# Strassen's scheme for the last 2048 tokens in two blocks, rows of x by head pairs through DRAM, and a third T tile

## The chip, the cores and the metric

The kernel runs on one core of a Trainium2 chip. The metric is the device time of one execution in microseconds (us), and the time of a kernel is the median of its runs. Engines are named as in the profile: PE (matmul), PEld (its weight loads), DVE (vector), ACT (scalar), POOL (GpSimd) and SP, which only issues DMAs here.

## The reference

Eight batches of eight heads, 576 positions, head size 64. Causal attention with a decay, then a feed-forward layer with a softplus over all 4608 tokens. Everything is float32.

```
scores = scale * np.matmul(q, k.transpose(0, 1, 3, 2))
cum = np.cumsum(np.log(np.clip(f, 0.0001, 1.0)), axis=-1)
scores = np.where(causal, -1000000000.0, scores + cum[:, :, :, None] - cum[:, :, None, :])
attn = softmax(scores)                       # exp(scores - max) / (sum + 1e-09)
x = matmul(attn, v) as [4608, 512]           # token by (head, head size)
h = x @ w_in                                 # 512 -> 2048
g = np.maximum(h, 0.0) + np.log1p(np.exp(-np.abs(h)))
out = g @ w_out                              # 2048 -> 512
```

## The kernel before

**Precision.** A product of two float32 matrices is made of three matmuls on rounded halves: high by high, high by low, low by high. So nearly every operand is first split: a copy gives the high part (`h`, ACT or DVE), and a subtraction gives the low part (`l`, DVE). Where a name ends in `h` or `l`, this is meant.

**Attention.** One job is one head of one batch. The first 14 jobs (batch 0, `plain`) are built otherwise; the other 56 (`whole`, batches 1 to 7, eight jobs each) are alike. A job loads q and k (`raw`) and v (`vr`), splits v into `vhl` (L785 is its low part), and builds a T tile [128, 4, 576]: the high part of q and k, the low part (L811), four moves of 144 KB inside SBUF (L814) and rows of the decay (L802, L805). It then makes scores in six pieces: two matmuls each (L859, L860) into a PSUM bank of the tag `att`, of which there are four, the row minimum with mask on DVE (L864) and the exponential on ACT (L903). The weights are scaled (L931, L933), turned by PE (L996), split into `ph` and `pl` (L1015, L1018), and multiplied with v (L1143). The result is added into x on ACT and DVE (L1193). Two T tiles take turns, by the job's number.

**x.** One batch of x is a tile [128, 4, 576]: plane g holds the heads 2g and 2g + 1, and 576 tokens. There are two such buffers (`x32`); they also hold the running sums of the decay at the start and the gated values of the last block at the end.

**Feed-forward.** The first 3584 tokens go in blocks: two of 128, one of 256 and six of 512 tokens (`WIDE`). A wide block splits x (L1285), makes 16 up products of 12 matmuls with 512 columns each (L1336, weights `wih` in SBUF and `wl` loaded per pair from DRAM), a gate of three ACT passes (L1369, L1372, L1375), a sum on DVE (L1383) and a split (L227, L1391), and 16 down products (L1423), of which half the tokens' values wait in DRAM (`g_d`, L1395 out, L1478 back) for a second pass. So a wide block is 192 up and 192 down matmuls.

**The last 1024 tokens** (`SUPER, NSUPER = 1024, 1`) are one block by Strassen's scheme in Winograd's form. Even and odd tokens are two halves of 512. Per pair of 128 hidden columns (`fp`, eight pairs) seven products of six matmuls stand where eight stood (L1856, banks A, B, C, D), with sums of weight quarters on POOL (L1738), sums of products on DVE (L1885) and four gates. The down products of the even tokens (L1978, banks E0 to E3) follow at once; the gated values of the odd tokens go to DRAM (`odd_d`, L1929) and come back in a tail (L2012) after the last product. `lay_x` makes the seven operands B11, T2, T1, T3, B21, B22, T4 from x in SBUF. They lie in tiles that attention has left (`late_raw`, `late_T`, `late_vhl`, `late_ph`, `late_pl`, `late_p`, `late_xl`).

**The order.** All engines' instructions are put in an order by a planner (`Plan.run`) with a cost for each operation; the engines then run their queues in that order and wait by semaphores. Operations wait in it for buffers by tag (`takes`, `give`), mostly first come first served. Feed-forward units are dealt out between the parts of the attention jobs by `share`. The last pass of the last wide block (`left`) stands between attention and the Strassen block.

## Time and profile before

| what | us |
|---|---|
| median of 3 runs (1135.66 to 1136.82) | 1136.08 |
| the profiled execution | 1137.25 |
| its span | 1135.4 |
| PE busy in the span | 1123.0 |
| DVE busy | 850.8 |
| ACT busy | 838.8 |
| POOL busy | 185.6 |

A row of a group reads: line, engine, operation, out<-in, partitions by elements, count, busy us, mean ns of one. The chain of waits names what the end of the program was waiting for at each moment. In a table by stretch, each engine has its busy us and, in brackets, its number of instructions. A matmul's record lasts longer than its share of PE, since the next begins before it ends; the distance of starts is the share.

### The profile page before, as it was taken

What the parts mean: (1) busy time and instruction counts of PE and PEld (TensorE: products, weight loads), DVE (VectorE), ACT (ScalarE), POOL (GpSimd) and SP (SyncE); (2) the same over time, 40 slices, a digit from 0 to 9 for tenths busy, and PEclk for the clock granted to TensorE, in tenths of its full rate; (3) what the DMA queues carried; (4) which work ended last, traced back from release to release, by engine and by line L of the source; (5) the groups of instructions that cost most, each with busy time, mean ns of one, the idle gap of its engine ahead of it and who ended that gap; (6) DMA issues with size and microseconds to landing.
All of it is one profiled execution on the core that took longest, in us unless ns stands there. A gap on an engine that the chain in (4) does not pass through costs nothing.

```text
span 1135.4 us, 19910 instructions
## 1 busy us (share of the span) xinstructions
PE 1123.0 (99%) x6230; PEld 939.8 (83%) x6230; DVE 850.8 (75%) x2131; ACT 838.8 (74%) x2033; POOL 185.6 (16%) x225
## 2 busy tenths in 40 slices
PE   9999999999999999999999999999999999999998
PEld 7766789888888888888888888888888888888887
DVE  7888999987787777777777778677867778867610
ACT  6888798889877777678767787677867875766610
POOL 3323221111111001000010000000000013555200
PEclk9999999999999999999999999999999999999999
DMA  8868676566575656666576466665657535322481
GB/s 244 252 183 229 179 215 163 148 174 175 158 208 159 174 164 175 161 186 170 151 203 189 137 179 182 165 179 158 174 153 208 142 99 162 130 93 98 162 278 38
DMA packets 160489, 192.97 MB, mean 170 GB/s; under 512 B 54944, under 2 KB 120768, under 8 KB 160384
## 3 DMA queue, kind: packets, MB, share of 16 engines
q1 hardware_dynamic: 160216, 191.55, 59.1%
q8 instruction: 50, 0.82, 0.3%
q14 instruction: 55, 0.45, 0.1%
q10 hardware_dynamic: 168, 0.15, 0.0%
HBM read 114.17 MB, written 44.34 MB: 140 GB/s over the span
## 4 chain that ended last, share of the span: by engine, by line
PE 86%; DVE 8%; ACT 3%; DMA 2%; issue 1%; SPq 0%; DVEq 0%
PE acc L1423 24%; PE h L1336 24%; PE b L996 7%; PE o L1143 7%; PE late_E L1978 4%; PE s L860 4%; PE s L859 4%; PE late_A L1856 2%; PE late_D L1856 2%; PE late_C L1856 2%; DVE s L864 1%; PE late_B L1856 1%; PE late_D L1978 1%; PE late_C L1978 1%; PE late_A L1978 1%
## 5 line engine op out<-in xcount | busy, mean ns | idle before, releaser
L864 DVE CUSTOM_DVE_ANT_0 s<-s,cmask 128x288 f32<-128x288 f32 (+6 forms) x320 | 137.1, 440 | 60.6 <-PE s L860 54.2
L903 ACT ACTIVATE pb<-s,negm 128x288 f32<-128x288 f32 (+5 forms) x272 | 143.3, 531 | 45.8 <-DVE negm L864 43.9
L933 POOL TENSOR_SCALAR pb<-pb,rsum 128x448 f32<-128x448 f32 (+2 forms) x44 | 59.5, 1353 | 415.8 <-ACT e L1375 192.9
L1336 PE MATMUL h<-xh,wl 128*128 128x512 f32 (+1 forms) x448 | 126.0, 380 | 0.0
L1336 PE MATMUL h<-xh,wih 128*128 128x512 f32 (+1 forms) x448 | 117.0, 383 | 0.5 <-DVE gl L1391 0.5
L1018 DVE TENSOR_TENSOR pl<-b,ph 128x512 fp32r<-128x512 f32 x168 | 107.1, 662 | 9.5 <-ACT ph L227 8.7
L1336 PE MATMUL h<-xl,wih 128*128 128x512 f32 (+1 forms) x448 | 113.9, 376 | 0.0
L227 ACT CAST ph<-b 128x512 fp32r<-128x512 f32 (+2 forms) x169 | 80.1, 492 | 34.8 <-PE b L996 33.1
L859 PE MATMUL s<-T 128*128 128x192 f32 (+1 forms) x336 | 99.3, 304 | 3.0 <-ACT pb L903 1.3
L1423 PE MATMUL acc<-woh_dt_float32r,gh 128*128 128x512 f32 x248 | 99.2, 400 | 0.0
L1369 ACT ACTIVATE e<-h 128x512 f32<-128x512 f32 x112 | 66.8, 596 | 43.3 <-PE h L1336 42.2
L860 PE MATMUL s<-T 68*128 68x192 f32 (+1 forms) x336 | 98.2, 296 | 0.0
L1423 PE MATMUL acc<-woh_dt_float32r,gl 128*128 128x512 f32 x248 | 97.4, 393 | 0.0
L1423 PE MATMUL acc<-wol_dt_float32r,gh 128*128 128x512 f32 x248 | 97.1, 392 | 0.0
L1336 PEld LDWEIGHTS h<-xl,wih 128*128 128x128 f32 x448 | 80.8, 188 | 16.6
L1336 PEld LDWEIGHTS h<-xh,wl 128*128 128x128 f32 x448 | 80.1, 189 | 13.0 <-issue 0.5
L1383 DVE SCALAR_TENSOR_TENSOR h<-h,e 128x512 f32<-128x512 f32 x104 | 73.3, 705 | 20.4 <-ACT e L1375 19.4
L1336 PEld LDWEIGHTS h<-xh,wih 128*128 128x128 f32 x448 | 77.8, 189 | 11.8 <-DVE gl L1391 0.7
L1143 PE MATMUL o<-ph,vhl 128*128 128x512 f32 x336 | 84.8, 290 | 0.0
L1391 DVE TENSOR_TENSOR gl<-h,gh 128x512 fp32r<-128x512 f32 x104 | 71.5, 687 | 16.0 <-ACT gh L227 14.6
L996 PE MATMUL b<-halves,pb 128*128 128x128 f32 x512 | 82.2, 272 | 0.0
L1372 ACT ACTIVATE e<-e 128x512 f32<-128x512 f32 x112 | 70.8, 632 | 1.9
(368 smaller groups left out, 2812.9 us busy)
## 6 DMA issues: line engine op xcount, KB each, us to landing
T<-T SPq DMA_DIRECT2D x224, 144.0 KB
wl<-wil_d SPq DMA_DIRECT2D x56, 512.0 KB
raw<-in_qkT SPq DMA_DIRECT2D x112, 144.0 KB
g_d<-gh SPq DMA_DIRECT2D x84, 128.0 KB
g_d<-gl SPq DMA_DIRECT2D x84, 128.0 KB
vr<-in_vR SPq DMA_DIRECT2D x64, 160.0 KB
out<-ob SPq DMA_DIRECT2D x28, 256.0 KB
sto<-in_w_out SPq DMA_DIRECT2D x11, 512.0 KB
```

Source lines behind the costliest of these rows:

```text
L227: (e.tensor_copy if hasattr(e, "tensor_copy") else e.copy)(out, in_)
L859: e.matmul(o, qA[:, S - end : S - q0], kA[:, a:z], start=True, stop=False)
L860: e.matmul(o, qB[0:ST, S - end : S - q0], kB[0:ST, a:z], start=False, stop=True)
L864: e.tensor_tensor_reduce(out=box["o"], in0=box["o"], in1=cmask[0:n_q, right - w : right], scale=-0.125, scalar=m0 if i else 3.0e38, op0=AL ...
L903: e.activation(o, box["o"], AF.Exp, bias=m1, scale=-1.0, accum_out=acc)
L996: e.transpose(box["ps"][0 : x.shape[1], at : at + one.shape[1]], x, one)
L1018: e.tensor_sub(box["l"], box["ps"][:, 0:w], box["h"].bitcast(F32))
L1143: e.matmul(boxes[gi]["ps"][0:m, a:z], st["vhl"][:, c, 0:m], pbox[which][:, o : o + z - a], start=gi in fresh and which == "h", stop=gi == ...
L1336: e.matmul(o, l, r, start=m == 0, stop=m == 11)
L1423: e.matmul(st["acc", tt], l, r[fc], start=first and m == 0, stop=last and m == 2,)
L1856: e.matmul(banks[to], stationary(x, j), at(b, y, j), start=start and m == 0, stop=m == 5, skip_group_check=not start,)
L1978: e.matmul(banks[x], l, r[fc], start=first and m == 0, stop=final and m == 2)
```

## The change

Strassen's scheme takes the last 2048 tokens, in two blocks of 1024, and the wide blocks are four and no longer six. The x of batches 2 to 7 is no longer kept by batches in SBUF: a buffer `xc` holds four planes (`xp`), an attention job writes into the plane of its head pair, and after every second job `store_x` sends that plane to DRAM (`x_d`, 288 KB). The wide blocks from token 1024 on load their x back by planes (256 KB, `split_stored`), and each Strassen block loads its x in two loads of 1 MB (`lay_x`). The other x buffer (`x0`) becomes a third T tile once batch 0 has been used. After attention both buffers (`big`) are used by turns for the loaded x of a Strassen block and for its gated even values. T tiles are taken as they come free. The low parts of T and `vhl` may now be made on POOL too. The tail of the first block takes the banks E0 and E1 for its second half, and its last eight units come after the second block's preparation, the last five of them ranked behind (`FILL`, `BEHIND`). The planner's costs for a DMA, and the shares by which feed-forward units are dealt out, are others.

```diff
-SUPER, NSUPER = 1024, 1
-BEHIND = 190
+SUPER, NSUPER = 1024, 2
+POOLB = 0.0
+BEHIND, FILL, REST, START = 190, 5, 4, 3
...
-                x32=2, ps=2, wl=2, vhl=3, vraw=1, raw=2, one=2)
-    plan = Plan(BUFS | dict(T0=4, stat=4, p=2, xh0=1, xh1=1, xl0=1))
+                xc=1, x0=1, ps=2, wl=2, vhl=3, vraw=1, raw=2, one=2)
+    plan = Plan(BUFS | dict(T0=4, xp=0, big=0, stat=4, p=2, xh0=1, xh1=1, xl0=1))
...
-            vl = add(subs(nv * D), v_lo, after=[vh])
+            vl = add([subs(nv * D), On("POOL", 0.2 + nv * D * 0.0022, POOLB, True)], v_lo, after=[vh])
...
-                t = T[number % 2]
+                st["at"] = T_free.pop(0)
+                t = T[st["at"]]
...
-            l_ = add(On("DVE", 0.75, 0.0, True), lo, after=[h_])
+            l_ = add([On("DVE", 0.75, 0.0, True), On("POOL", 0.2 + S * 0.0022, POOLB, True)], lo, after=[h_])
...
-            give("T", st["scores"])
+            give("T", st["scores"], lambda: T_free.append(st["at"]))
...
+    def store_x(b, g):
+
+        def store(e):
+            e.dma_start(out=x_d[g, :, b * S : (b + 1) * S], in_=plane(b, g))
+
+        need = [d for _, _, d, g_ in wrote[b] if g_ == g]
+        stores[b, g] = add_dma(store, 288, after=need)
+        if b > 1:
+            done = add(NO_ENGINE, mark, after=[stores[b, g]])
+            give("xp", [done], lambda: xp_free.append(x_of[b, g]))
...
+        def split_stored():
+            ready, low = [], []
+            for cc in range(NCC):
...
+                    e.dma_start(out=box["x"], in_=x_d[cc, :, t0 : t0 + nt])
...
+                if b == 0 and lo + w == S:
+                    give("x0", splits[0])
+                    third = add(NO_ENGINE, mark, takes=("x0",), lag=0.0)
+                    set_rows(2, [third])
+                    give("T", T_set[2], lambda: T_free.append(2))
...
+            give("big", [add(NO_ENGINE, mark, takes=("xp",) * NCC, lag=0.0)], lambda: big_free.append("xc"))
+            give("big", [add(NO_ENGINE, mark, takes=("T",), lag=0.0)], lambda: big_free.append("x0"))
...
+                def load(e, j=j, xbox=xbox):
+                    xbox["at"] = big_free.pop(0)
...
+                    e.dma_start(
+                        out=xbox["x"],
+                        in_=x_d[j : NCC : 2, :, t0 : t0 + SUPER].rearrange("c p t -> p c t"),
+                    )
+
+                ld = add_dma(load, 1024, after=stored(t0, SUPER, (j, j + 2)), takes=("big",))
...
+                if fc in (NFC - 3, NFC - 1):
+                    k = fc // 2 % 2
+                    give("big", [o], lambda: big_free.append(g_room["at", k]))
...
-            one = tail(["B", "A"], 0, False)
-            two = tail(["C", "D"], 2 * P, s == NSUPER - 1)
+            end = s == NSUPER - 1
+            spots = [(x, j) for x in OPERANDS[: 7 if end else 2] for j in range(2)]
+            one = tail(["B", "A"], 0, spots, False)
+            two = tail(["E0", "E1"], 2 * P, spots, end)
...
-        share = sum(c for c, _ in ffn) / (until - n + 1 + DELAY) / max(1, len(units))
+        here = sum(c for c, _ in ffn)
+        share = here / (until - n + 1 + (START if n <= nstart + H else DELAY))
...
+        whole_ = n - 1 - nstart
+        if n > nstart and whole_ % 2 == 1:
+            store_x(1 + whole_ // H, whole_ % H // 2)
...
-        for i, (_, unit) in enumerate(left):
-            plan.late = BEHIND * (i >= len(left) - 5)
+        for i, unit in enumerate(left):
+            plan.late = BEHIND * (i >= len(left) - FILL)
             unit()
-        plan.late, left = 0, []
-        for unit in units:
+        plan.late, left = 0, units[len(units) - 8 :]
+        for unit in units[: len(units) - 8]:
             unit()
+    for unit in left:
+        unit()
```

Two places show the order of the queues. The first is SP's queue where attention ends and the first Strassen block begins: `gh`/`gl` are the loads of the last wide block's second pass, `x_d` is x in DRAM, `late_x` the loaded x of a Strassen block, `late_wl` its weights. Before, the block's x is in SBUF and nothing is loaded for it:

```order
L1722 DMA late_wl0_1_11361<-wil_d_96 128x1024
L1478 DMA gh8_0b_11416<-g_d_97 128x2x256
L1478 DMA gl8_0b_11418<-g_d_97 128x2x256
L1235 DMA out_0<-ob8_0_11432 128x512
L1235 DMA out_0<-ob8_1_11443 128x512
L1478 DMA gh8_1b_11511<-g_d_97 128x2x256
L1478 DMA gl8_1b_11513<-g_d_97 128x2x256
```

Now, in SP's queue at the same place, the last plane of batch 7 is stored and the second load of x comes behind two more loads of the second pass:

```order
L1563 DMA gh6_3b_10279<-g_d_97 128x2x256
L1563 DMA gl6_3b_10281<-g_d_97 128x2x256
L1248 DMA x_d_98<-xp_2909 128x576
L1563 DMA gh6_4b_10335<-g_d_97 128x2x256
L1563 DMA gl6_4b_10337<-g_d_97 128x2x256
L1563 DMA gh6_5b_10360<-g_d_97 128x2x256
L1563 DMA gl6_5b_10362<-g_d_97 128x2x256
L1720 DMA late_x2560_1_10365<-x_d_98 128x2x1024
L1563 DMA gh6_6b_10383<-g_d_97 128x2x256
```

What moved: the store of x and the two loads of x are new in this queue, and the second load stands between the loads that PE's cover needs.

The second place is PE's queue where a Strassen block's first product stands (`late_A` to `late_D` are its banks, `acc` and `late_E` those of down products). Before, there is one such place, behind the second pass of the last wide block:

```order
L1423 MATMUL acc8_3_11494<-woh9_dt_float32r_1523,gh8_4b_11610 128x512
L1423 MATMUL acc8_3_11494<-wol9_dt_float32r_1555,gh8_4b_11610 128x512
L1423 MATMUL acc8_3_11494<-woh9_dt_float32r_1523,gl8_4b_11612 128x512
L1856 MATMUL late_A_11380<-late_raw1_10993,wih_95 128x512
L1856 MATMUL late_A_11380<-late_T0_11158,wih_95 128x512
```

Now PE's queue has a second such place: the second block's first product (bank C) stands in the first block's tail, whose values `gho` have come back from DRAM:

```order
L2058 MATMUL late_A_10028<-woh13_dt_float32r_1577,gho0_0_6_11570 128x512
L2058 MATMUL late_A_10028<-wol13_dt_float32r_1909,gho0_0_6_11570 128x512
L2058 MATMUL late_A_10028<-woh13_dt_float32r_1577,glo0_0_6_11572 128x512
L1937 MATMUL late_C_10288<-late_T1_10018,late_xh0_10005 128x512
L1937 MATMUL late_C_10288<-late_vhl0_10088,late_xh0_10005 128x512
```

What moved: this product was nowhere before, and 36 matmuls of the first block's tail stand between it and the first block's last down product.

More of the change, by code (lines that the diff above doesn't have):

```diff
@@ L95, in start_of @@
             n, free = op.takes.count(tag), self.free[tag]
-            early = self.queue[tag][0] is not op
+            head = self.queue[tag][0]
+            early = 0 if head is op else head.takes.count(tag) if EARLY else 1
             if len(free) < n + early or (early and not op.loose):
+                return None
+            if early and op.guard and op.guard.end is None:
                 return None
@@ L126, in run @@
                 op.lag = SEEN[eng]
+            if op.kb:
+                self.moved = max(self.moved, op.start + ISSUE) + op.kb / RATE
+                op.lag = max(0.0, self.moved - op.end) + LAND
             if on.port:
@@ L1218, in attention, with plane, stored @@
         )
-    splits = {}
+    splits, stores = {}, {}
+    def plane(b, g):
+        return x_of[b][:, g, :] if b < 2 else xp["x"][:, x_of[b, g], :]
+    def store_x(b, g):
[6 more added lines that the diff above has]
+            give("xp", [done], lambda: xp_free.append(x_of[b, g]))
+    def stored(t0, n, planes=range(NCC)):
+        return [stores[b, g] for b in range(t0 // S, (t0 + n - 1) // S + 1) for g in planes]
     kept_read = {}
@@ L2036, in step @@
                     loads["used", fp].append(o)
+                    if not spots_of[fp] and tiles[-1] == k == 1:
+                        give("gh", [o])
+                        give("gl", [o])
                     return o
@@ L2242, in tile_decay_attention_softplus_ffn @@
         until = min((at for at in ready_at if at >= n), default=n)
-        share = sum(c for c, _ in ffn) / (until - n + 1 + DELAY) / max(1, len(units))
+        here = sum(c for c, _ in ffn)
+        share = here / (until - n + 1 + (START if n <= nstart + H else DELAY))
+        if n > nstart + H:
+            later = sum(NFC * on_pe(WIDE, 24).cost for x in ready_at.values() for _ in x)
+            share = min(share, (here + later) / (len(jobs) - n + REST))
+        share /= max(1, len(units))
         credit = 0.0
```

219 lines of the change are left out of this document (127 added, 92 removed).

## The prediction

> **What bounds the kernel now.** I read the page first, then the busy times by stretch, then the chain of waits by stretch. The page:
>
> ```profile
> span 1135.4 us, 19910 instructions
> PE 1123.0 (99%) x6230; PEld 939.8 (83%) x6230; DVE 850.8 (75%) x2131; ACT 838.8 (74%) x2033; POOL 185.6 (16%) x225
> ```
>
> PE is busy for all but 12.4 us. A record of a matmul overlaps the next one, so that share hides small waits, but it leaves no large one. Busy us by stretch (start:end, length, then each engine):
>
> ```profile
> 100.00:150.00 50.00, 47.51 (x314) 35.22 (x313) 46.07 (x122) 40.79 (x104) 12.65 (x15) 1.00 0.74 203
> 150.00:250.00 100.00, 99.14 (x644) 87.36 (x643) 90.95 (x245) 89.70 (x238) 16.36 (x15) 1.00 0.65 173
> 250.00:300.00 50.00, 50.00 (x281) 42.72 (x279) 38.28 (x102) 43.26 (x110) 4.43 (x4) 1.00 0.59 161
> 250.00:950.00 700.00, 698.49 (x3825) 594.13 (x3822) 528.44 (x1349) 540.08 (x1335) 62.34 (x60) 1.00 0.60 168
> 950.00:1100.00 150.00, 150.00 (x663) 123.87 (x662) 100.04 (x182) 88.36 (x169) 57.62 (x75) 1.00 0.44 151
> ```
>
> From 250 to 950 attention and wide blocks are mixed: PE idles 1.5 us of 700, DVE is at 75% and ACT at 77%. From 950 on the Strassen block runs with no idle PE at all. In the denser stretch from 150 to 250 DVE is at 91%, ACT at 90%, and PE idles 0.86 us of 100. The chain of waits of the mixed stretch, then that of the dense one:
>
> ```profile
> by line: PE h L1336 35.9%; PE acc L1423 34.4%; PE o L1143 9.7%; PE b L996 9.3%; PE s L860 5.0%; PE s L859 4.8%; issue 0.1%; ACT pb L903 0.1%; DVE x L1193 0.1%; DVE xl L1285 0.1%; DVE s L864 0.1%; ACT ph L227 0.1%; ACT x L227 0.1%; ACT pb L9
> ```
>
> ```profile
> by line: PE h L1336 20.0%; PE acc L1423 19.4%; PE b L996 9.2%; PE o L1143 7.5%; PE s L859 4.4%; DVE pl L1018 4.3%; PE s L860 4.2%; DVE s L864 3.7%; issue 3.3%; DVE gl L1391 2.1%; ACT pb L931 2.0%; DVE h L1383 1.8%; DVE wil L575 1.8%; ACT x
> ```
>
> In the mixed stretch the path is PE alone (99%). In the dense one PE has 65% of it; the rest runs through DVE and ACT. So today the kernel is its matmuls, and fewer matmuls are less time as long as the other engines keep up.
>
> **The matmuls.** Pieces of the chain (start, us, count):
>
> ```profile
> 438.30 2.77 PE acc L1423 x12
> 489.39 2.76 PE h L1336 x12
> 950.32 12.29 PE acc L1423 x54
> 962.60 1.36 PE late_A L1856 x6
> 987.39 5.44 PE late_E L1978 x24
> ```
>
> In the mixed stretch a matmul of 512 columns takes 2.77/12 = 0.2308 us of PE, in the Strassen block 1.36/6 = 5.44/24 = 0.2267. The change drops two wide blocks: 2 x (192 + 192) = 768 matmuls, 177.3 us. It adds a second Strassen block: 8 x 42 = 336 products and 384 down matmuls, 720 x 0.2267 = 163.2 us. Together **-14.1 us**: 48 matmuls fewer (10.9 us), and 720 at the faster pace. The order of the queues agrees: 5879 matmuls before, 5832 now (one more that fills a gap). I take the whole 14.1; if the pace belongs to the neighbours and not to the place, it is 10.9.
>
> **The second block's sums and gates.** They load DVE, ACT and POOL as the first block's do: 67%, 59% and 38% of the stretch from 950 to 1100, with PE at 150.00 of 150. I cost them at nothing; PE's 15 us per pair of columns hides them.
>
> **The attention that loses its cover.** How many jobs ran in a stretch shows in the score matmuls (L859, six a job; PE busy and count first):
>
> ```profile
> 150.00:250.00 100.00, 15.41 (x52) 9.35 (x52) 1.00 0.65 173
> 250.00:950.00 700.00, 77.17 (x266) 47.96 (x266) 1.00 0.60 168
> ```
>
> From 250 to 950 there are 266/6 = 44.3 jobs, 15.8 us each. Without two wide blocks the same jobs stand in 700 - 177 = 523 us, 11.8 us each; in the dense stretch it was 100/(52/6) = 11.5 us. So attention will run nearly everywhere at the pace that it has now only there. The work that leaves with the blocks, and that which goes to POOL (mean ns of one):
>
> ```profile
> L1383 DVE SCALAR_TENSOR_TENSOR h<-h,e 128x512 f32<-128x512 f32 x104 | 73.3, 705 | 20.4 <-ACT e L1375 19.4
> L1391 DVE TENSOR_TENSOR gl<-h,gh 128x512 fp32r<-128x512 f32 x104 | 71.5, 687 | 16.0 <-ACT gh L227 14.6
> L1369 ACT ACTIVATE e<-h 128x512 f32<-128x512 f32 x112 | 66.8, 596 | 43.3 <-PE h L1336 42.2 <-PE h L1315 0.7
> L1372 ACT ACTIVATE e<-e 128x512 f32<-128x512 f32 x112 | 70.8, 632 | 1.9
> L1375 ACT ACTIVATE e<-e 128x512 f32<-128x512 f32 x112 | 70.5, 629 | 1.7
> L811 DVE TENSOR_TENSOR T<-raw,T 128x576 fp32r<-128x576 f32 x56 | 42.3, 755 | 0.2
> L785 DVE TENSOR_TENSOR vhl<-vr,vhl 128x384 fp32r<-128x384 f32 x56 | 31.7, 565 | 1.2 <-ACT vhl L227 0.6
> L227 ACT CAST gh<-h 128x512 fp32r<-128x512 f32 x84 | 49.3, 586 | 23.2 <-DVE h L1383 21.1 <-PE s L860 0.8
> ```
>
> DVE loses 32 gates x (0.705 + 0.687) = 44.5 us, and by the order 22 of L811 and 32 of L785 go to POOL, 34.7 us: 528 - 79 = 449 of 523, 86%. ACT loses 32 x (0.596 + 0.632 + 0.629) = 59.4 us and some 26 of the casts (15 us): 540 - 75 = 465, 89%. That is just under the dense stretch. PE's idle time there, 0.86 per 100 us, makes 4.5 us over 523, where 1.5 stand today: **+3.0 us**. The bounds: nothing, as from 250 to 300, where ACT is at 87% and PE at 50.00 of 50; and the row from 100 to 150, DVE 92%, PE idle 2.49 of 50, which would be 26.0 - 1.5 = +24.5. I take the dense stretch, since it holds the same jobs at the same pace, and its loads are the nearest.
>
> **Third T tile.** The waits of SP's queue from 250 to 950 (us, times, longest):
>
> ```profile
> SPq L802 <- PE s L860: 57.7, 31, 5.5
> SPq L814 <- DMA T<-T: 40.8, 39, 3.5
> ```
>
> SP waits for a T tile to come free before it loads the decay rows (L802); behind it in the queue stand the gate's stores (L1395) and the next weights (L1307). With three tiles this wait goes; the next to come late are the moves (L814), each waiting for the one before. PE did not wait for T in these 700 us, so I give no gain. At best it and POOL's help return the 3.35 us that PE idles from 100 to 250; that is the low end.
>
> **Entering the Strassen blocks.** Now x comes from DRAM. DMAs on the path, from issue to landing, 256 KB and 512 KB; then the steps ahead of and behind them:
>
> ```profile
> 1.36 4.09 DMA T<-in_qkT
> 10.55 6.02 DMA sti<-in_w_in
> ```
>
> ```profile
> L1193 DVE TENSOR_TENSOR x<-o,x 64x512 f32<-64x512 f32 x56 | 38.4, 686 | 3.2 <-ACT x L227 1.6
> L227 ACT COPY x<-o 64x512 f32<-64x512 f32 x56 | 32.4, 578 | 0.7
> L1018 DVE TENSOR_TENSOR pl<-b,ph 128x512 fp32r<-128x512 f32 x112 | 76.7, 685 | 7.4 <-ACT ph L227 6.8
> ```
>
> The second half of the first block's x can only be loaded once the planes of batch 7 have been stored: 0.58 + 0.69 for the last output, 4.1 for the store (as 256 KB), a load of 1 MB, and 0.59 + 0.69 for the first split. The two rows differ by 1.93 us for 256 KB, so 1 MB is 4.09 + 3 x 1.93 = 9.9 us; without other traffic I guess at least 7. That is 13.6 to 16.5 us. PE's cover is the 60 matmuls that stand between the last output and the first product, 60 x 12.29/54 = 13.7 us: 0 to 2.8 us late, I take 2. Before, the 54 matmuls covered all. The second block's second load waits for the last even down product of the first; 7 to 9.9 us and three steps (0.69 + 0.59 + 0.69) stand against 36 matmuls, 8.2 us: 0.8 to 3.7 late, I take 2. Together **+4 us**, between 0 and 6.5.
>
> [...]
>
> **Sum.** 1137.25 - 14.1 + 3.0 + 4.0 = 1130.15 for the profiled execution, 7.1 less. The median lies 1.17 below it: 1136.08 - 7.1 = **1129.0**.
>
> **Rivals.**
> *All hidden* (22%). PE stays as full as from 250 to 300, and the loads land in time: 1136.08 - 14.1 = 1122, and up to 1125 with one entry or a little idle time. For it: 1.5 us of idle PE in 700 today. Against: the dense stretch.
> *The entries eat it* (10%). The loads of the second pass stand ahead of x in SP's queue; if each of x's two late loads also waits for 512 KB of theirs, that is 2 x 2 x 1.93 = 7.7 us, and -14.1 + 3 + 4 + 7.7 = +0.6, 1136.7: no change. For it: the queue's new order, and no slack in the covers. Against: those loads are issued earlier and may have landed by then.
> *POOL and DVE block one another* (6%).
>
> ```profile
> L507 DVE TENSOR_SCALAR ti<-ti x16: 407/422/1024, 14.2 to 103.3; 128x512 f32<-128x512 f32 x16
> L1738 POOL TENSOR_TENSOR p<-wih x16: 737/739/857, 930.9 to 1057.9; 128x256 f32<-128x256 f32 x16
> ```
>
> This DVE step takes 0.42 us, and up to 1.02 (min, median, max). At POOL's 0.739 us for 256 columns, the 54 subtractions there are 22 x 1.66 + 32 x 1.11 = 72 us. If DVE's steps on SBUF operands (11% of its time: L811 and L785, 0.755 + 0.565 of 11.8 us a job) meet them in proportion, some 8 us of DVE are lost; if PE waits for all of it, 1129 + 8 = 1137, no change. [...] Against: DVE would only go from 86 to 88%.
> *Attention is bound by DVE and ACT* (15%, slower). With less cover, each wait for a minimum, an exponential or a split reaches PE, as from 100 to 150: -14.1 + 24.5 + 4 = +14.4, 1150. It makes the kernel slower from an idle share of 1.3 us per 50 (13.9 of 523 us, against today's 1.5). For it: 35% of the dense chain is not PE. Against: PE idles only 0.43 per 50 in that stretch, although weights are still being split in it (L575 in its chain).
>
> **Numbers.** My forecast, 1125 to 1133.8, has 47%. About 0.2% (2.3 us) is what a measurement can tell here. Faster, below 1133.8: 47 + 22 + 1 = 70%. Same, to 1138.4: the entries' case and POOL's, 10 + 6 less that 1, 15%. Slower: 15%. The range reaches from just under the all-hidden time, leaving out the lowest end (1122 - 3.35), over both cases of no change to the start of the last rival, most of which it leaves out: 1121 to 1139.
>
> **What would show it.** The late products at 0.227 us a matmul and 672 of them; PE idle of 3 to 6 us between 250 and the last score; DVE near 86% and ACT near 89% there; a gap of 1 to 4 us ahead of the first product of each block, ended by work on `late_x`. I am wrong if PE idles by more than 14 us in attention, or a block's entry by more than 5, or if the chain of the mixed stretch is no longer PE.

## The result, and the profile after

The changed kernel takes 1152.88 us (median of 4 runs, 1150.58 to 1156.20) against 1136.22 for the kernel before on the same chip: a ratio of 1.0149, 95% interval 1.0121 to 1.0177. It is slower by 16.7 us, where I forecast 7 us faster. Its profiled execution took 1151.53 us. The head of its page:

```profile
span 1149.7 us, 20085 instructions
PE 1127.5 (98%) x6184; PEld 935.8 (81%) x6184; DVE 873.8 (76%) x2157; ACT 852.5 (74%) x2072; POOL 304.2 (26%) x350
```

46 recorded matmuls fewer, and 4.5 us more of busy PE: less work stands further apart. Busy us by stretch, first the mixed stretch of attention and wide blocks, then the first Strassen block:

```profile
250.00:800.00 550.00, 542.27 (x3097) 457.06 (x3096) 451.17 (x1224) 455.79 (x1203) 115.08 (x102) 1.00 0.69 189
850.00:950.00 100.00, 100.00 (x443) 82.81 (x442) 76.92 (x126) 69.54 (x124) 49.73 (x63) 1.00 0.43 143
```

The Strassen block is as full as before. In the mixed stretch PE idles 7.7 us of 550, where it was 1.5 of 700. That looks harmless; the chain of waits of the same stretch does not:

```profile
by line: PE h L1421 22.2%; PE acc L1508 21.5%; PE b L1012 9.1%; PE o L1159 8.6%; PE s L874 5.4%; PE s L875 4.5%; ACT pb L919 3.4%; DVE pl L1034 2.8%; issue 2.7%; ACT pb L947 1.6%; DVE s L879 1.4%; ACT e L1457 1.4%; ACT xp L236 1.4%; DMA T<-
```

PE has 71% of the path (the six PE entries), where it had 99% before. What PE's instructions waited for between 215 and 800 us (total us, times, longest), the changed kernel and then the one before:

```profile
PE o L1159 <- DVE pl L1034: 2.2, 3, 1.0
PE s L874 <- ACT p L919: 1.5, 5, 0.4
PE s L874 <- DMA T<-T: 1.4, 1, 1.4
PE b L1012 <- ACT pb L919: 1.4, 5, 0.4
```

```profile
PE s L859 <- ACT ph L227: 0.9, 1, 0.9
PE h L1336 <- DVE gl L1391: 0.5, 1, 0.5
```

Output matmuls wait for the low part of the weights (VectorE), scores wait for a PSUM bank that an exponential must empty (ScalarE), and once for a move into T. The rows hold only the waits that leave PE without a record.

**Where the time went.** Four rows of the two timelines mark the stages: the first score of job 22 and the first Strassen product, before and after.

```profile
211.99 0.19 PE L859 MATMUL s<-T 128*64 128x64 f32 x1
962.44 0.39 PE L1856 MATMUL late_A<-late_raw,wih 128*128 128x512 f32 x1
```

```profile
211.84 0.19 PE L874 MATMUL s<-T 128*64 128x64 f32 x1
814.12 0.39 PE L1937 MATMUL late_A<-late_raw,wih 128*128 128x512 f32 x1
```

Between them the order of PE's queue gives the number of feed-forward and Strassen matmuls. They are priced at the tenth percentile of their start-to-start time in the kernel before: 0.226 us for 512 columns, 0.117 for 256, and 0.2267 in the Strassen part. The 256-column ones belong to the block of 256 tokens; 24 of its up products now come behind the first score of job 22.

| stage | time, before and after | matmuls fewer or more | their work | lost |
|---|---|---|---|---|
| start to job 22 | 212.0, 211.8 | 12 fewer, and 24 of 256 columns fewer | -5.5 | 5.4 |
| job 22 to the first Strassen product | 750.4, 602.3 | 744 fewer, and 24 of 256 columns more | -165.3 | 17.2 |
| from there to the end | 173.0, 335.6 | 708 more | +160.5 | 2.1 |
| sum | 1135.4, 1149.7 | 48 fewer | -10.3 | 24.6 |

So 10.3 us of work went and 24.6 us of waiting came: +14.3 (figures rounded). Most of it is in attention, about a fifth in the start, and hardly any in the Strassen blocks.

For the experiments I use one measure of attention's waiting, the *excess*: over all PE records from the first score of job 22 to the first Strassen product, the time from each start to the next, less the tenth percentile of that tile and shape in the kernel before. Before it is 64.5 us, after 81.1 (the expectations say 65.5, counted with marks a little apart). The rise of 16.6 agrees with the 17.2 of the table. Each excess is from one execution. By pairs of neighbours, score to score rose from 5.1 to 12.9 us and output to output from 6.5 to 11.1: the two waits of the rows above. Of these 12.4 us more, 4.7 are gaps between records; the rest is too short to leave one.

Other points of the prediction. The late products, pieces of the chain in the Strassen part:

```profile
835.83 1.36 PE late_A L1937 x6
837.19 2.72 PE late_E L2058 x12
807.01 7.20 DMA late_x<-x_d
```

0.2267 us a matmul, as forecast, and the load of 1 MB landed in 7.20 us, where I had 9.9 and at least 7. No gap stood ahead of either block's first product; the first block has three of 0.4 to 0.7 us within its first 21 us. The third tile moved most of SP's wait as forecast, from the T tile to the moves into it (SP's queue, 250 to 800; L816 loads the decay rows, L802 before):

```profile
SPq L828 <- DMA T<-T: 51.2, 41, 4.0
SPq L816 <- PE b L1012: 18.2, 24, 2.2
```

**The start.** A table of 4 us slices of the changed kernel, from 64 us on (the number behind POOL's count is the granted clock):

```profile
64.00:68.00 4.00, 3.79 (x28) 2.71 (x28) 3.67 (x13) 3.70 (x8) 2.65 (x4) 1.00 1.04 293
68.00:72.00 4.00, 1.86 (x17) 0.98 (x13) 3.92 (x9) 3.09 (x7) 1.17 (x2) 0.85 0.67 169
72.00:76.00 4.00, 4.00 (x18) 3.64 (x18) 3.50 (x10) 4.00 (x12) 0.73 (x2) 0.50 0.04 11
```

PE stands still for 2.14 us, and then the granted clock is halved. The trace also holds the moments at which it changes, and two stretches before job 22 are at half clock:

```profile
70.78:77.61 6.83, 6.64 (x26) 5.75 (x27) 4.66 (x12) 5.97 (x16) 2.13 (x3) 0.50 0.21 62
16.17:19.58 3.41, 3.41 (x16) 2.93 (x15) 3.38 (x12) 3.41 (x11) 2.50 (x4) 0.50 0.97 367
```

For 10.24 us in all PE has half its clock, and matmuls of 128 columns (L1400, L2283) start 0.213 us apart in these stretches, where it is 0.112 elsewhere: by my estimate up to 5.1 us lost. In the kernel before the clock is at 1.00 from 4 us on until its last 2 us. What PE waited for at 69 us shows in the timeline (start, us; the last bracket is idle time):

```profile
68.55 0.98 DVE L520 TENSOR_SCALAR ti<-ti 128x512 f32<-128x512 f32 x1
69.45 0.51 DVE L879 CUSTOM_DVE_ANT_0 s<-s,cmask,negm 128x288 f32<-128x288 f32 x1
70.22 0.65 DVE L1114 TENSOR_TENSOR x<-o,p 64x192 f32<-64x192 f32 x2
70.97 0.87 PE L869 MATMUL s<-T 66*128 66x320 f32 x1 [2.14 <-issue]
```

The scores start 0.10 us behind the end of L1114 (70.87), which empties the outputs' PSUM bank; before it VectorE still splits weights (L520) and takes a minimum. The profile calls the wait "issue", so that releaser is my reading, not a row.

### The profile page after: what moved, and what is told of

Its sections match the earlier page's. It is cut to its first block, busy times and chain, and to the rows that moved or that the text cites. A ratio compares the mean times of both kernels' runs of the same rounds, so it can differ in the third digit from the quotient of the medians.

```text
span 1149.7 us, 20085 instructions
## 1 busy us (share of the span) xinstructions
PE 1127.5 (98%) x6184; PEld 935.8 (81%) x6184; DVE 873.8 (76%) x2157; ACT 852.5 (74%) x2072; POOL 304.2 (26%) x350
## 4 chain that ended last, share of the span: by engine, by line
PE 74%; DVE 10%; ACT 9%; DMA 4%; issue 2%; SPq 1%; POOL 0%; DVEq 0%; ACTq 0%; POOLq 0%
PE h L1421 13%; PE acc L1508 12%; PE late_E L2058 10%; PE b L1012 6%; PE o L1159 5%; PE late_C L1937 3%; PE late_D L1937 3%; PE late_A L1937 3%; PE s L874 3%; PE s L875 3%; PE h L1400 2%; PE acc L1527 2%; ACT pb L919 2%; PE late_B L1937 2%; PE s L869 1%
## 5 line engine op out<-in xcount | busy, mean ns | idle before, releaser
L1421 PE MATMUL h<-xh,wl 128*128 128x512 f32 (+1 forms) x320 | 92.3, 377 | 0.0
L2058 PE MATMUL late_E<-woh_dt_float32r,late_g 128*128 128x512 f32 x256 | 82.6, 389 | 0.0
L1421 PE MATMUL h<-xh,wih 128*128 128x512 f32 (+1 forms) x320 | 81.5, 376 | 0.4 <-DVE gl L1476 0.4
L874 PEld LDWEIGHTS s<-T 128*128 128x128 f32 (+1 forms) x336 | 60.5, 180 | 24.5 <-ACT p L919 7.3
L1421 PE MATMUL h<-xl,wih 128*128 128x512 f32 (+1 forms) x320 | 79.3, 370 | 0.0
L947 ACT ACTIVATE pb<-pb,rsum 128x320 f32<-128x320 f32 (+2 forms) x120 | 73.9, 654 | 0.1
L825 POOL TENSOR_TENSOR T<-raw,T 128x576 fp32r<-128x576 f32 x22 | 31.5, 1432 | 147.5 <-ACT T L236 78.2
L1159 PE MATMUL o<-pl,vhl 128*128 128x512 f32 x224 | 67.5, 345 | 2.3 <-DVE pl L1034 2.2
L1159 PEld LDWEIGHTS o<-ph,vhl 128*128 128x128 f32 x336 | 63.4, 189 | 6.6 <-DVE pl L1034 0.2
L875 PEld LDWEIGHTS s<-T 68*128 68x128 f32 (+1 forms) x336 | 60.5, 180 | 10.0 <-issue 2.0
```

The lines of the kernel that those rows point to most:

```text
L874: e.matmul(o, qA[:, S - end : S - q0], kA[:, a:z], start=True, stop=False)
L875: e.matmul(o, qB[0:ST, S - end : S - q0], kB[0:ST, a:z], start=False, stop=True)
L1159: e.matmul(boxes[gi]["ps"][0:m, a:z], st["vhl"][:, c, 0:m], pbox[which][:, o : o + z - a], start=gi in fresh and which == "h", stop=gi == ...
L1421: e.matmul(o, l, r, start=m == 0, stop=m == 11)
L2058: e.matmul(banks[x], l, r[fc], start=first and m == 0, stop=final and m == 2)
```

## The experiments

Theory: with a third of the wide products gone, attention's chain (scores, minimum, exponential, split, output) has too little PE work beside it, and the load of VectorE and ScalarE reaches PE. Rivals: POOL's new splits, x through DRAM, the third T tile, the planner's new rules. All times are medians with the ratio to the kernel before on the same chip.

### Taking products away, and putting them back

**x1_before_four_wide**, in the kernel before:

```
-    BLOCKS += [(t, WIDE) for t in range(SHORT, NT - NSUPER * SUPER, WIDE)]
+    BLOCKS += [(t, WIDE) for t in (512, 1536, 2048, 3072)]
...
-                if lo + w == S:
-                    give("x32", splits[b])
+                if lo + w == S or at + w in (1024, 2560):
+                    give("x32", splits[b] + [d for _, _, d, _ in wrote[b]])
```

> The kernel before, with two of its six wide FFN blocks (tokens 1024 to 1535 and 2560 to 3071) left out and nothing else: no Strassen block more, no third T tile, no x through DRAM. [...] Theory (the attention's own chain of scores, minimum, exponential and split loses cover when FFN products are taken away): 1137 - 168 + 16 = 985 us, 980 to 995, and between the first score of job 22 and the first Strassen product PE is 14 us or more over the pace of its matmuls beyond what it was (65.5). Rivals (POOL's new work, x through DRAM, or the third tile costs it): none of them is in this kernel, so 1137 - 168 = 969 us, 966 to 973.

Measured: 1020.38 us, ratio 0.898 (0.8965 to 0.8995), excess 120.0. That is 51 us above the rivals' 969, and 35 above my own 985: right in sign, far too small. No run shows the 168 us in these sums: for 768 matmuls that is 0.219 us each, and the shortest start-to-start of two up products in the kernel before is 0.224. At 0.226 the rivals' time is 962, and the run lies 58 us above it. Two slices of its profile, around the start of job 34:

```profile
356.00:360.00 4.00, 2.29 (x16) 1.74 (x14) 3.77 (x14) 2.63 (x8) 0.00 (x0) 1.00 0.33 77
364.00:368.00 4.00, 3.54 (x13) 2.73 (x12) 2.94 (x10) 2.99 (x9) 1.25 (x1) 0.50 0.44 111
```

With blocks 2 and 5 left out the products don't spread evenly: jobs 34 to 37 and 61 have none at all. Jobs 22 to 68 by the time that their feed-forward matmuls take:

| feed-forward us in the job | jobs | mean us of a job | mean excess |
|---|---|---|---|
| none | 5 | 10.1 | 6.7 |
| under 5 | 7 | 11.2 | 4.6 |
| 5 to 8 | 12 | 11.1 | 1.5 |
| 8 to 10 | 12 | 13.7 | 1.6 |
| over 10 | 11 | 15.9 | 1.3 |

In this run a job without products is only about 1 us shorter than one with 5 to 8 us of them, so taking these away saves little; batch 3 alone has 34.6 us of excess (10.3 before). That isn't a floor for every job: in the changed kernel six jobs with under 5 us of products, each between fuller ones, took 8.5 us with 1.5 us of excess. Part of the loss is clock: between job 22 and the first Strassen product the granted clock is at 0.50 for 44 us, up to 22 us lost. What waits is mostly what waits in the changed kernel:

```profile
PE b L996 <- ACT pb L903: 10.3, 16, 1.1
PE s L859 <- ACT p L903: 8.3, 13, 1.0
```

Behind these waits the chain from 355 to 380 runs through the moves into T first (17.6%), with two T tiles. Thin cover alone, without any other part of the change, costs 51 us or more here; it is thinner in places than in the changed kernel, so the size doesn't carry over, the mechanism does.

**x2_after_denser**, in the changed kernel, with each half of an up product of the wide blocks issued twice, 768 matmuls of 512 columns more and no more work on any other engine (the sums come out twice too large):

```
-                for m in range(6 * half, 6 * half + 6):
-                    l, r = todo[m]
-                    e.matmul(o, l, r, start=m == 0, stop=m == 11)
+                for n in range(12 if wide else 6):
+                    l, r = todo[6 * half + n % 6]
+                    e.matmul(o, l, r, start=half == 0 and n == 0, stop=half == 1 and n == (11 if wide else 5))
```

> [...] Theory (lost cover): the attention's chain is covered again, the excess over the matmuls' pace falls back to about 65 us, and the time is 1151.5 + 168.1 - 16 = 1303 us, 1298 to 1308. Rivals (POOL's work, x through DRAM, third tile): these are all still there, 1319 us, 1314 to 1324.

Measured: 1313.04 us, ratio 1.1557 (1.1535 to 1.1578), between the two. A matmul of an up product costs 0.226 us, so 768 of them are 173.6 us; no run shows the 168.1 of these sums. From job 22 to the first Strassen product 602.3 + 173.6 = 775.9 was due and 762.9 measured. The excess fell to 68.1, by 13.0 of the 16.6. The chain from 250 to 950:

```profile
by line: PE h L1421 47.8%; PE acc L1508 20.9%; PE o L1159 9.3%; PE b L1012 8.8%; PE s L874 5.0%; PE s L875 4.7%; issue 0.6%; DVE pl L1034 0.4%; DMA T<-T 0.4%; ACT xp L236 0.2%; DVE xl L1324 0.2%; DVE ph L236 0.2%; ACT pb L947 0.2%; ACT pb L
```

PE has 96% of the path again, with POOL's splits, x through DRAM and the third tile all in place and nothing moved on the other engines. More cover hides most of the waiting. It would hide waits that those parts of the change make as well, so this run doesn't clear them; x3, x4 and x13 ask about them one by one.

### POOL's splits and the third tile

**x3_no_pool_split**:

```
-POOLB = 0.0
+POOLB = 1000.0
```

> The changed kernel with the low parts of T and of V never on POOL (a bias that the planner never takes), as before. Rival (POOL's 1.4 us splits are late, or block VectorE): most of the 16 us come back, 1136 to 1143 us. Theory (lost cover): VectorE gets some 22 T splits and the V splits back, its share rises, and the time stays or rises, 1150 to 1160 us.

Measured: 1164.83 us, ratio 1.0248 (1.0223 to 1.0272), excess 92.6: 12 us slower than the changed kernel. POOL's help is real, a little more than I allowed. The planner laid out all queues anew in this run and in the next; x9 and x13 below show that this alone can cost some 5 us.

**x4_two_T**:

```
-                    third = add(NO_ENGINE, mark, takes=("x0",), lag=0.0)
-                    set_rows(2, [third])
-                    give("T", T_set[2], lambda: T_free.append(2))
...
-            give("big", [add(NO_ENGINE, mark, takes=("T",), lag=0.0)], lambda: big_free.append("x0"))
+            give("big", [add(NO_ENGINE, mark, takes=("x0",), lag=0.0)], lambda: big_free.append("x0"))
```

> The changed kernel without the third T tile (its room stays empty until the Strassen blocks take it). If the third tile with its new order of scores is what costs: 1138 to 1146 us. Theory (lost cover, for which the third tile is a help): 1152 to 1160 us, with waits for the moves into T between the scores of one job and the next.

Measured: 1171.32 us, ratio 1.0304 (1.0278 to 1.0331), excess 94.1: 18 us slower. I had given the third tile no gain; under thin cover it is worth some 18 us, a part of which may be the new layout. The waits that I named did not come, though; those for ScalarE and VectorE grew:

```profile
PE s L874 <- ACT p L919: 2.4, 4, 1.1
PE o L1159 <- DVE pl L1034: 2.3, 4, 0.7
```

**x11_before_pool_split**, the kernel before with the same choice for both low parts:

```
-            vl = add(subs(nv * D), v_lo, after=[vh])
+            vl = add([subs(nv * D), On("POOL", 0.2 + nv * D * 0.0022, 0.0, True)], v_lo, after=[vh])
...
-            l_ = add(On("DVE", 0.75, 0.0, True), lo, after=[h_])
+            l_ = add([On("DVE", 0.75, 0.0, True), On("POOL", 0.2 + S * 0.0022, 0.0, True)], lo, after=[h_])
```

> The kernel before, with POOL allowed to take the low parts of T and of V, as in the changed kernel, and nothing else. In the changed kernel this is worth 12 us. Theory: that help counts only where the cover is thin; under six wide blocks PE sets the time, 1134 to 1139. If the splits on POOL are good by themselves: 1130 or less; if a POOL split is late by itself: 1140 or more.

Measured: 1140.86 us, ratio 1.0048 (1.0029 to 1.0067). Worth 12 us under thin cover, the same edit costs 4 under full cover: no gain, as the theory says, but the small loss I had only as the last case. The excess rose from 64.5 to 67.3, all of it in batch 2.

### Sparing the two engines

**x5_light_act, x6_light_dve, x7_light_both** (the first edit, the second, both), and **x8_before_light_both** (both, in the kernel before):

```
             def exp(e):
-                e.activation(box["e"], box["e"], AF.Exp, scale=-1.0)
+                w = slice(0, 64 if wide else 512)
+                e.activation(box["e"][:, w], box["e"][:, w], AF.Exp, scale=-1.0)
...
-                e.activation(box["e"], box["e"], AF.Ln, bias=1.0)
+                w = slice(0, 64 if wide else 512)
+                e.activation(box["e"][:, w], box["e"][:, w], AF.Ln, bias=1.0)
```

```
-                e.scalar_tensor_tensor(h, h, 0.0, box["e"], ALU.max, ALU.add)
+                w = slice(0, 64 if wide else 512)
+                e.scalar_tensor_tensor(h[:, w], h[:, w], 0.0, box["e"][:, w], ALU.max, ALU.add)
```

> The changed kernel, its order untouched; in the gates of the four wide blocks the exponential and the logarithm run over 64 of 512 columns (the gates are wrong). ScalarE loses 64 x 2 x some 0.4 us, about 51 us, no other engine anything. If ScalarE's load is what makes the exponentials of the scores late, so that scores wait for their PSUM banks: the excess between the first score of job 22 and the first Strassen product falls from 81 to 70 us or less, 1141 us, 1136 to 1146. If VectorE's load is the cause, or the length of the chain itself whatever the load: under 4 us, 1148 to 1153.

> The changed kernel, its order untouched; in the same gates VectorE's sum runs over 64 of 512 columns (64 x some 0.5, 32 us less on VectorE). If VectorE's load is what makes minima and splits late: the excess falls to 73 us or less, 1144 us, 1139 to 1148. If it is ScalarE's load or the length of the chain: under 4 us, 1148 to 1153.

> Both edits in the changed kernel. If the load of the two engines is the cause: the excess falls to the 65 us of before, 1136 us, 1131 to 1141. If it is the length of the chain at any load: 1147 to 1153.

> Both edits in all six wide blocks of the kernel before, as the control. Theory: PE's own matmuls set the time there, so the excess stays at 62 to 65 us and the time at 1133 to 1137, whatever the two engines are spared. If lighter gates help any kernel alike (through the entry of the late part or the start), it gains as much as the changed one, 10 us or more: 1126 or less.

| run | us | ratio (95%) | excess |
|---|---|---|---|
| changed kernel | 1152.88 | 1.0149 (1.0121 to 1.0177) | 81.1 |
| x5_light_act | 1145.60 | 1.0087 (1.0070 to 1.0104) | 74.4 |
| x6_light_dve | 1148.93 | 1.0116 (1.0091 to 1.0141) | 75.6 |
| x7_light_both | 1142.86 | 1.0062 (1.0042 to 1.0082) | 73.2 |
| kernel before | 1136.22 | 1 | 64.5 |
| x8_before_light_both | 1135.83 | 0.9994 (0.9980 to 1.0009) | 63.6 |

The stretch from 250 to 800 and its chain with both edits:

```profile
250.00:800.00 550.00, 544.80 (x3133) 465.08 (x3132) 433.20 (x1233) 417.71 (x1207) 116.94 (x104) 1.00 0.69 192
by line: PE h L1421 28.1%; PE acc L1511 26.5%; PE o L1159 11.0%; PE b L1012 10.8%; PE s L874 6.0%; PE s L875 5.7%; DMA T<-T 2.2%; DMA xp<-x_d 1.6%; DMA late_x<-x_d 1.4%; issue 1.1%; ACT pb L947 0.9%; DVE pl L1034 0.9%; ACT xp L236 0.6%; ACT
```

ScalarE has 38 us less to do there and VectorE 18 (455.79 and 451.17 in the changed kernel), PE's share of the path rises from 71 to 88%, and the time falls by 10.0 us. The control gains nothing. So the load of the two engines is a cause, and only where cover is thin. But the excess gives back 7.9 of 16.6, not all, and x5 to x7 miss the theory's bounds for it (70, 73 and 65): the load is a part of the cause. Sparing either engine alone gives most of it (6.7 and 5.5), and the gains don't add; that would fit two links of one chain, but isn't shown to be it. In batch 4, where five jobs in a row have 36 feed-forward matmuls each (8.1 us), the excess of 1.46 us a job fell to 1.18, the level of the kernel before. The other 8.7 us stay. Job 34 alone has 4.7 us more than in the kernel before and job 22 has 2.1, the rest being small gains and losses. In job 34 of x7, ScalarE and then PE:

```profile
363.91 0.62 ACT L236 CAST xh<-xp 128x512 fp32r<-128x512 f32 x1 [0.89 <-DMA xp<-x_d]
364.44 0.49 ACT L919 ACTIVATE pb<-s,negm 128x288 f32<-128x288 f32 x1
365.07 0.32 PE L1012 MATMUL b<-ident,p 68*128 68x68 f32 x1 [1.35 <-ACT pb L919]
```

ScalarE stands for a load of x from DRAM, and the exponential that PE needs stands behind the split of that x. Two us earlier the same happens once more, and the clock is at 0.50 from 365.18 to 368.59, up to 1.7 us more. In the changed kernel ScalarE comes to these splits later and doesn't wait for the loads; the exponentials stand behind the splits all the same. So x through DRAM is a rival for a part of what is left.

### x through DRAM

**x9_store_twice** and **x13_store_twice_same_order**:

```
+        again = add_dma(lambda e: e.dma_start(out=x2_d[g, :, b * S : (b + 1) * S], in_=plane(b, g)), 288, after=need)
...
-            done = add(NO_ENGINE, mark, after=[stores[b, g]])
+            done = add(NO_ENGINE, mark, after=[stores[b, g], again])
```

```
             e.dma_start(out=x_d[g, :, b * S : (b + 1) * S], in_=plane(b, g))
+            e.dma_start(out=x2_d[g, :, b * S : (b + 1) * S], in_=plane(b, g))
```

> The changed kernel with every plane of x stored a second time, to another place in DRAM that nobody reads: 28 stores of 288 KB more in SP's queue during attention. If x through DRAM (its traffic, or SP's queue behind the stores) is a part of what attention lost, that part comes once more: 5 us or more, 1157 to 1165. Theory (load of VectorE and ScalarE under thinner cover): 1150 to 1156, with the excess of attention within 2 us of 81.

> Again every plane of x stored twice, but now both stores stand together in SP's queue and the planner does not know of the second: the order on PE, VectorE, ScalarE and POOL is that of the changed kernel, word for word. In the run before, which cost 8 us, the planner had laid out all anew. If the stores themselves (traffic, SP's queue) cost attention: 1157 to 1163 again, excess 86 or more. If it was the new layout: 1150 to 1156, excess 79 to 84.

Measured: 1160.42 us, ratio 1.0211 (1.0191 to 1.0231), excess 90.5, and 1154.99, ratio 1.0157 (1.0124 to 1.0190), excess 83.7. The first looked like a verdict against my theory; the second shows that most of it was the new layout of all queues. The stores themselves cost some 2 us a set, within the spread of the runs. No run varies the loads of x back into SBUF, for which ScalarE waits in x7.

### The start, and the planner's rules

**x10_shifted_stream**:

```
+        for _ in range(30):
+            e.matmul(o[:, 0:8], halves, halves[:, 0:8], start=True, stop=True)
```

> The changed kernel with 30 matmuls of 8 columns more in the warm-up, ahead of everything: they cost PE under 2 us there and move all that follows by 30 matmuls in PE's instruction stream; order and waits stay. In every run of the changed family PE stands still for 2.1 us ahead of the same scores near 69 us, for nothing that the profile shows, and the granted clock is at 0.5 for some 8 us behind it. If the place in the instruction stream makes that stall: it is gone from there, the clock stays at 1.00 from 72 to 80, and job 14 begins at 113 to 115 instead of 118.1; 1146 to 1151. If something else of the kernel makes it (a DMA, a semaphore): the same scores wait 2.1 us again, 1151 to 1156.

Measured: 1168.21 us, ratio 1.0278 (1.0259 to 1.0297). The 30 small float32 matmuls cost not under 2 us but 9.75, and the granted clock was 0.5 from 9.6 to 36.9 us. Yet it answers the question: the same scores still stand 2.14 us, now at 87.0 us, and the clock falls behind them:

```profile
6.27 9.75 PE L2273 MATMUL warm<-halves 128*128 128x8 f32 x60
```

```profile
84.00:88.00 4.00, 1.64 (x18) 0.83 (x13) 3.92 (x9) 3.09 (x7) 1.21 (x2) 1.00 0.58 162
88.00:92.00 4.00, 3.60 (x18) 3.60 (x19) 3.54 (x10) 4.00 (x12) 0.79 (x2) 0.57 0.00 0
```

It is a wait of the program, not the place in the stream.

**x14_start_as_before**:

```
-BEHIND, FILL, REST, START = 190, 5, 4, 3
+BEHIND, FILL, REST, START = 190, 5, 4, 2
```

> The changed kernel with the share of FFN products in the start, up to job 22, handed out as before (START = 2 in place of 3). The changed kernel enters job 22 at the same time as before, but with 36 matmuls of the first wide block fewer behind it, 8.1 us of work, and with the stall at 69 us and the halved clock behind that. If the thinner share is what lost these 8 us: job 22 begins at 212 us with 30 matmuls or more caught up, and the time is 1145 to 1149 us. If the stall has other causes (the order of the loads, VectorE's splits): it is still there, 1150 to 1158.

Measured: 1155.49 us, ratio 1.0172 (1.0150 to 1.0194). The stall at 69 us is gone, another of 3.55 us has come, up to 41.37, and the clock fell behind that one:

```profile
36.00:40.00 4.00, 1.82 (x12) 1.24 (x10) 3.93 (x12) 3.87 (x9) 2.07 (x3) 1.00 0.95 247
40.00:44.00 4.00, 2.63 (x4) 1.14 (x5) 4.00 (x8) 2.78 (x7) 2.16 (x3) 0.79 1.01 318
```

Job 22 began at 214.2 us, with the 36 matmuls caught up. As 24 of them have 256 columns, they are 5.5 us of work and not the 8.1 of the expectation. That gives back 3.2 of the 5.4 us, but the excess of attention is 90.5, with those products no longer beside it, and the time as long as that of the changed kernel.

**x12_no_portions**:

```
-PAIR = 1.4
+PAIR = 0.0
```

> The changed kernel, FFN products handed out between attention's units one by one and not in portions of at least 1.4 us (PAIR = 0). With both engines lightened, 8.7 us of the excess of 16.6 were left, in single waits of about 1 us in jobs that hold 4 to 6 us of FFN products. If those come from where the products stand among attention's units, this spread changes the excess by 4 us or more, down to 77 or less: 1145 to 1149. If they come from the mean cover alone, the excess stays at 79 to 83, 1150 to 1156.

Measured: 1151.38 us, ratio 1.0126 (1.0109 to 1.0143), excess 83.3. No change that can be told: this spread is not it.

**x15_before_new_dma_price**, in the kernel before:

```
+            if op.kb:
+                self.moved = max(self.moved, op.start + ISSUE) + op.kb / RATE
+                op.lag = max(0.0, self.moved - op.end) + LAND
...
-    return On(eng, max(0.6 * n, kb / RATE) if eng == "SP" else 1.5 * n)
+    return On(eng, (ISSUE if eng == "SP" else 1.5) * n)
...
-        return add(on_dma(kb, n, eng), emit, lag=dma_lag(kb, n, eng), **more)
+        op = add(on_dma(kb, n, eng), emit, lag=LAND, **more)
+        op.kb = kb
+        return op
```

> The kernel before, with one thing of the changed planner: its price of a DMA (0.4 us on the queue, then all transfers one after the other, and 1.9 us to land). This lays out the loads of the start anew; blocks, tiles and engines stay. If this price is what loses the changed kernel its 8 us in the start: PE stalls by 1 us or more ahead of job 14, the granted clock falls below 1.00 behind it, and the time is 1140 to 1146 us. If the loss comes from the rest (POOL, the share, the thinner cover): job 22 begins at 212 us as before with as much work done, 1134 to 1138 us.

Measured: 1147.05 us, ratio 1.0098 (1.0077 to 1.0119). A price in the planner, with no work added and hardly any moved (VectorE has six instructions fewer, ScalarE and POOL three more each), costs the kernel before 10 us. The slices from 12 us on show the first hole, in this kernel and then in the one before:

```profile
12.00:16.00 4.00, 2.97 (x21) 2.07 (x20) 2.14 (x9) 2.90 (x8) 1.24 (x2) 0.90 0.92 321
16.00:20.00 4.00, 4.00 (x16) 3.29 (x13) 3.97 (x12) 3.09 (x10) 2.15 (x4) 0.50 1.04 387
```

```profile
12.00:16.00 4.00, 4.00 (x25) 2.65 (x24) 3.51 (x15) 2.65 (x8) 1.06 (x2) 1.00 0.88 279
16.00:20.00 4.00, 3.41 (x29) 2.59 (x28) 3.08 (x10) 3.34 (x9) 2.68 (x4) 1.00 1.01 386
```

The changed kernel has the same hole:

```profile
12.00:16.00 4.00, 3.06 (x22) 1.91 (x20) 1.61 (x6) 2.48 (x8) 0.77 (x1) 1.00 0.95 340
16.00:20.00 4.00, 4.00 (x21) 3.52 (x21) 3.86 (x12) 3.96 (x11) 2.89 (x5) 0.57 0.95 356
```

The stall at 69 us is not in this kernel, so the price alone doesn't make that one. The excess is 71.3, 5.7 of the rise of 6.8 in batch 2. The granted clock is at 0.50 from 15.24 to 22.06 us and from 223.45 to 230.28, where batch 2 begins: up to 6.8 us of lost clock, as much as the profiled execution lost (6).

**x16_old_dma_price** and **x17_old_price_no_portions** put the old price (the lines with - above) into the changed kernel, the second with `PAIR = 0.0` as well:

> The changed kernel with the planner's old price of a DMA, all else as changed. The new price alone cost the kernel before 10 us (more of it behind job 14 than ahead). If it costs the changed kernel as much: 1141 to 1146 us, with the excess of attention at 72 to 77 and the start without its stall. If that was one unlucky layout, and any new layout of the thin stretch is about as good: 1150 to 1158 us.

> The same, with FFN products handed out one by one (PAIR = 0). In the changed kernel that was worth 1.5 us at most. The same bounds: 1139 to 1146 us if the price is the cause; 1148 to 1158 if it is not. Under 1134 it would beat the kernel before, which only the first theory allows, and that barely.

Measured: 1148.97 us, ratio 1.0109 (1.0092 to 1.0125), excess 80.6, between the two bounds, and 1144.83, ratio 1.0073 (1.0056 to 1.0090), excess 76.8. So the price is worth about 4 us in the changed kernel, not 10, and 8 together with the other spread. In x16 the new layout also took 43 instructions off VectorE, so it is the layout with all that follows from it that gains. Further, the hole at 12 us is gone in x16, the stall is not; it stands at 66 us there:

```profile
12.00:16.00 4.00, 4.00 (x29) 2.79 (x28) 2.68 (x12) 2.91 (x11) 1.23 (x4) 1.00 0.85 262
...
64.00:68.00 4.00, 1.92 (x20) 1.20 (x20) 3.99 (x10) 2.89 (x7) 2.13 (x3) 1.00 0.99 267
68.00:72.00 4.00, 3.82 (x13) 2.92 (x14) 3.84 (x10) 4.00 (x12) 0.97 (x1) 0.52 0.84 272
```

The better of the two is still 8 us slower than the kernel before; no run here points to a version that beats both.

## Why the prediction was wrong

**The bound today: right.** x8 shows it best: sparing VectorE and ScalarE in the kernel before changes nothing. But I read "fewer matmuls are less time as long as the other engines keep up" and then sized the condition wrongly.

**The matmuls: work right, gain not.** 48 matmuls fewer are 10.9 us, and the late products run at 0.2267 us as forecast. The other 3.2 us, "720 at the faster pace", came in part: the excess between one up product and the next and one down product and the next fell from 14.1 to 12.3 us. But the excess of attention as a whole did not fall with these products gone, it rose.

**The attention that loses its cover: the step that failed.** "PE's idle time there, 0.86 per 100 us, makes 4.5 us over 523, where 1.5 stand today: +3.0 us." The mechanism was there, and so were the loads: I had 86% and 89% over 523 us, and they are 82 and 83% of the 550 that were measured. The size was wrong: 17.2 us (16.6 by the excess), more than five times as much. Idle time between records is not what PE waits. A record of a matmul lasts 0.39 us while the next one starts 0.226 us after it, so that a wait of 0.1 us leaves no gap. In the changed kernel 7.7 us of idle time in 550 stand for the larger loss. I had written of this overlap at the first row, and then priced by idle time all the same. The weight loads show the loss in direction: PEld fell from 594.13 of 700 us (84.9%) to 457.06 of 550 (83.1%), and in x7 it is back at 465.08 (84.6%). Better would have been pace: how much longer the dense stretch takes than its matmuls.

**The rival that held.** "Attention is bound by DVE and ACT", 15%, gave 1150 us; 1152.9 came. Its mechanism, that each wait for a minimum, an exponential or a split reaches PE, is what the waits, x2 and x5 to x8 show. That its price of 24.5 us came out near the total is luck in part: 17.2 us are in attention, and 5.4 in the start, which it did not speak of. My test for being wrong, an idle PE of more than 14 us in attention, would have passed this kernel (7.7 us, where I had 3 to 6); the other one, that the chain is no longer PE's, caught it.

**The start: a term that was missing.** I read the stretch from 100 to 250 for its loads only and took all before it as unchanged, although new prices and shares lay out its queues anew. It lost 5.4 us: a hole of 0.94 us near 14 and one of 2.14 near 70, and behind them a halved clock, up to 5.1 us.

**The entries: the first right in size, the second too dear.** 2.1 us were lost in the whole Strassen part, 4 forecast. All of it lies in the first block, behind its first product and not ahead of it; the second block's entry, for which I had 2, cost nothing.

**Third T tile and POOL: undersized.** I gave the tile nothing and POOL's splits only a relief of VectorE. They are worth some 18 and 12 us in the changed kernel, new layouts included; without them it would be far worse. They help against the thin cover that the same change makes.

**POOL and DVE blocking one another: a little.** VectorE's own T splits tell nothing of it: none of the 34 ran beside an instruction of POOL, since the planner (its `port`) keeps such pairs apart. But the small sums `lsum` do meet POOL's splits (min, median, max in ns; two rows of the changed kernel, then one of the kernel before):

```profile
L825 POOL TENSOR_TENSOR T<-raw,T x22: 1408/1436/1447, 131.3 to 703.8; 128x576 fp32r<-128x576 f32 x22
L932 DVE SCALAR_TENSOR_TENSOR lsum<-lsum,part x70: 145/156/1028, 11.3 to 793.4; 128x5 f32<-128x5 f32 x56, 128x3 f32<-128x3 f32 x8, 128x2 f32<-128x2 f32 x4, 128x4 f32<-128x4 f32 x2
```

```profile
L916 DVE SCALAR_TENSOR_TENSOR lsum<-lsum,part x70: 144/166/168, 10.3 to 940.8; 128x5 f32<-128x5 f32 x56, 128x3 f32<-128x3 f32 x8, 128x2 f32<-128x2 f32 x4, 128x4 f32<-128x4 f32 x2
```

Five of them, from 167 us on, took 0.45 to 1.03 us beside a split of T or V on POOL, and each ended within 0.03 us of it: some 3 us of VectorE in all, where that rival had 8. Those 8 took each meeting as lost to VectorE in full, which was my estimate.

**What stays open.** Of attention's 16.6 us of excess, 13.0 come back with thicker cover and 7.9 with lighter engines; the 8.7 that lighter engines leave are not explained. The loads of x from DRAM stand ahead of two waits of PE in x7 and are untested, and no run separates the planner's rules one by one. Each new layout brings its own holes, and with them stretches at half clock, so a difference of a few us between two layouts says little of the part that was changed. In the start, the wait at 69 us is named by reading the timeline, not by an experiment. That x15 costs 10 us by the median while its profiled execution is only 6 longer than that of the kernel before is not explained.

## What to carry to other kernels

Work on the bounding engine is also cover for the chains beside it: before some of it is moved to another stage, find how much cover each job needs there, by pace (time of the stretch against its matmuls) and not by idle time. Here 10 us of matmuls saved were not worth a third of the cover of 48 jobs. A new price in a planner is a change of its own, to be timed alone: here it was worth 4 to 10 us. So is any edit that lets the planner lay out anew: x9 and x13 add the same stores and differ by 5 us.

## What the runs showed of the hardware

Behind some short holes PE's granted clock was halved, behind others it was not. In the changed kernel it was 0.50 for 3.41 us (from 16.17) behind a hole of 0.94 us (13.58 to 14.52) and for 6.83 us behind the one of 2.14 us. A hole of 1.43 us there (218.73 to 220.16) left it at 1.00, and so did one of 1.15 us in the kernel before (112.84 to 113.99). In x1 it was at 0.50 for some 13.6 us behind a hole of 1.09 us (up to 359.69), by the slices of 4 us from 360 to 376 (0.77, 0.50, 0.50, 0.53); in x16 it was 0.52 from 68 to 72 us, behind 2.26 us without a record of PE between 64 and 72. What decides it isn't shown. The single wait at 70 us was 2.14 us long, and with up to 3.4 us of lost clock behind it (half of the 6.83) it cost more than twice its length.

In x9 the trace has 0.95 wherever others have 1.00, yet PE's stretch from 900 to 950 us, in the Strassen part, holds 222 matmuls, as many as in x10 at 1.00.

Small float32 matmuls were dear: 30 of 8 columns made 60 records in 9.75 us in x10, and the slice from 12 to 16 us, at a granted clock of 0.50, holds 20 of them.
